# Norm of x moved from VectorE to ScalarE, both heads' first exponentials sent to SBUF, and a new list of order refinements, in an attention plus two-MLP kernel

## The chip, the cores and the metric

The kernel runs on one core of one Trainium2 chip. The metric is device time in microseconds (us) of one execution. Before the change the median of three runs is 991.84 us (990.38 to 995.52).

## What is computed

Causal attention with a decay bias feeds two MLP layers without bias or residual. Batch 4, 8 heads, 576 positions, head dimension 64; the 2304 token rows have 512 columns.

```
scores = q @ k^T / 8 ; bias = -(cum_i - cum_j) ; cum = cumsum(max(s, 0))
scores = where(causal, -1e9, scores + min(bias, 0))
attn   = exp(scores - rowmax) ; attn /= sum(attn) + 1e-9
x      = (attn @ v), heads side by side            # 2304 x 512
h = x @ w_in ; x = (h - tanh(h)) @ w_out           # d_ff 2048
x = ((x @ w_a) * (x @ w_b)) @ w_out2               # d_ff 1536
```

## The kernel before, in words

All large products run in fp16 on TensorE (PE). To keep the precision, an fp32 operand is scaled by a power of two and split into a high and a low fp16 part (`copy_scaled` makes the high one, `lo_part` the low one), and three products stand for one. The scale comes from a norm of the operand: `w_split`, `g_square` and `x_norm` each reduce the squares of a tile to one value for each partition, a tiny matmul with ones adds these up over the partitions, and `pow2` (L735) cuts the result to a power of two with five short VectorE (DVE) instructions.

**Attention** goes by units: one batch and one pair of heads, first with the first two 128-row query tiles (4 x 4 units), then with the last two and the 64-row tail ("merged" units, 4 x 4). In a unit, for each of the two heads `h` and each query tile `t`, `u_qk` (L1002) puts scores into a PSUM bank, a DVE instruction adds the causal mask and takes the row extreme `nm`, `u_exp` (L1045) takes the exponential on ScalarE (ACT) with its row sum `sm`, `u_rec` inverts the sums, and `u_norm` (L1059) scales and splits the result into `a`, which a transposing DMA turns for the product with v. The exponential normally overwrites its PSUM bank. For head 1's first query tile (`t == u.ts[ZSB]`, with `ZSB = 0`) it goes to a tile `zs` in SBUF instead, of which each of the two pools holds two. GpSimd (POOL) cannot be given work on a PSUM bank here, so the flag `ps` in L1068 leaves it out of the choice for `copy_scaled` and `lo_part` where the data stand in PSUM.

**First MLP**: nine blocks of 256 token columns, the first on fp32 weights without a split, the other eight on split operands. At the head of such a block `x_norm` (L1107) finds the norm of the block's x with a DVE instruction (a fused multiply and reduce by max, `sq,xmx`) and four accumulating tiny matmuls, `x_split` makes the fp16 parts, and `gel_scale` (L1125) works out the block's scales (`xc1`, `xt`, `xsg`, `xik`) with short DVE instructions. Then come eight steps of `l1_mm`, `l1_act` (tanh on ACT, the rest on DVE), `l2_mm`. **Second MLP**: `l3_*`, `l4_mm`, and from its third block on a form with seven products for eight (`seven*`), for which `a_sums` and `b_sums` add up sub-matrices into tiles `xf`, `sq`, `x2hl`.

**Order.** Every operation is recorded with a due time (`due`), and a planner (`Plan.run`, L382) issues them engine by engine from its own cost figures. Operations inside `pl.either()` carry several engines, and the planner takes the one that it reckons to be done first; `small` (L926) is such a choice between DVE and POOL. Operations that share a port between POOL and DVE are marked by `shares` and take turns. `REFINE` (L38) is a list of 33 steps; each runs the plan, goes back from its end, and moves the due times towards the latest ones, with random shifts drawn from the step's last number. So a change in any operation or in this list changes the order on all engines.

Of the kernel before, what the change touches and what calls it, by code (L numbers as in the profile page):

```python
# [13 lines left out]
BF16 = mybir.dt.bfloat16  # L14
# [4 lines left out]
AF = mybir.ActivationFunctionType  # L19
ALU = mybir.AluOpType  # L20
# [14 lines left out]
MASKED = -1.0e34  # L35
BLOCKS = [(p, [b]) for p in range(2) for b in range(4)]
TURN = 0.0
REFINE = [(2000.0, 0.1, 300.0, 103), (0.0, 0.2, 1000.0, 287), (0.0, 0.2, 0.0, 206), (400.0, 0.05, 300.0, 66365), (2000.0, 0.1, 300.0, 492), (-200.0, 0.05, 1000.0, 826), (400.0, 0.05, 300.0, 3748), (200.0, 0.2, 1000.0, 456), (-200.0, 0.5, 300.0, 21796), (200.0, 0.0, 300.0, 72166), (0.0, 0.1, 1000.0, 999), (0.0, 0.7, 1000.0, 66510), (2000.0, 0.05, 3000.0, 472), (2000.0, 0.0, 2000.0, 530), (200.0, 0.0, 3000.0, 76843), (100.0, 0.05, 2000.0, 663), (200.0, 0.2, 1000.0, 93186), (0.0, 0.0, 300.0, 851), (100.0, 0.0, 3000.0, 40468), (200.0, 0.2, 0.0, 78025), (2000.0, 0.2, 0.0, 26040), (400.0, 0.05, 2000.0, 38163), (400.0, 0.2, 1000.0, 715), (2000.0, 0.2, 0.0, 319), (2000.0, 0.1, 300.0, 15767), (-200.0, 0.05, 2000.0, 47989), (200.0, 0.2, 0.0, 999), (-200.0, 0.0, 2000.0, 43198), (400.0, 0.05, 0.0, 60058), (200.0, 0.1, 0.0, 58400), (0.0, 0.7, 1000.0, 951), (0.0, 0.2, 1000.0, 27296), (100.0, 0.0, 300.0, 65696)]  # L38
SEVEN = 12
GSB = (1,)  # L40
ZSB = 0
# [590 lines left out]
def tile_attention_two_moes(  # L632
# [20 lines left out]
    KD = DM // P  # L653
# [51 lines left out]
    ones16 = fixed.tile([P, P], BF16, name="ones16")  # L705
# [29 lines left out]
    def pow2(src, n, inv, sc=None):  # L735
        nn = new("moe", [P, 8], F32, "p2n", 4)
        aa = new("moe", [P, 8], I32, "p2a", 4)
        pl.vector.tensor_scalar_max(nn[:, :n], src, TINY)
        pl.vector.tensor_scalar(
            out=aa[:, :n], in0=nn[:, :n].bitcast(I32), scalar1=24, scalar2=23,  # L740
            op0=ALU.logical_shift_right, op1=ALU.logical_shift_left,
        )
        pl.vector.tensor_scalar_mul(inv, aa[:, :n].bitcast(F32), DN)
        if sc is not None:
            bb = new("moe", [P, 8], I32, "p2b", 4)
            pl.vector.tensor_single_scalar(out=bb[:, :n], in_=aa[:, :n], scalar=EXPO, op=ALU.bitwise_xor)
            pl.vector.tensor_scalar_mul(sc, bb[:, :n].bitcast(F32), UP)
# [32 lines left out]
    def lo_part(out_, in_, sc, hi, psum=False):  # L780

        if psum:
            pl.vector.scalar_tensor_tensor(out=out_, in0=in_, scalar=sc, in1=hi, op0=ALU.mult, op1=ALU.subtract)
            return
        with pl.either():
            pl.vector.scalar_tensor_tensor(out=out_, in0=in_, scalar=sc, in1=hi, op0=ALU.mult, op1=ALU.subtract)
            with pl.group():
                if not isinstance(sc, float) or sc != 1.0:
                    pl.gpsimd.tensor_scalar(out=in_, in0=in_, scalar1=sc, scalar2=1.0, op0=ALU.mult, op1=ALU.mult)
                pl.gpsimd.tensor_tensor(out=out_, in0=in_, in1=hi, op=ALU.subtract)  # L790
# [29 lines left out]
    def copy_scaled(out_, in_, sc, psum=False):  # L820
        with pl.either():
            pl.scalar.activation(out=out_, in_=in_, func=AF.Copy, scale=sc)
            pl.vector.tensor_scalar_mul(out_, in_, sc)
            if not psum:
                pl.gpsimd.tensor_scalar(out=out_, in0=in_, scalar1=sc, scalar2=1.0, op0=ALU.mult, op1=ALU.mult)
# [173 lines left out]
    def col(u, h, t):  # L999
        return 2 * u.nq if h == 2 else h * u.nq + u.ts.index(t)  # L1000
# [41 lines left out]
    def span(u, h, t):  # L1042
        return (0, NT + 1) if h == 2 else (u.zoff[t], t + 1)

    def u_exp(u, h, t):  # L1045
        c = col(u, h, t)
        zz = u.ztail if h == 2 else u.pq[h, t]
        to = zz
        if h == 1 and t == u.ts[ZSB]:
            to = u.pq[h, t] = anew(u, [P, (u.ts[ZSB] + 1) * P], F32, "zs")  # L1050
        pl.scalar.activation(
            out=to, in_=zz, func=AF.Exp, scale=-1.0, bias=u.nm[:, c:c + 1], accum_out=u.sm[:, c:c + 1])
# [6 lines left out]
    def u_norm(u, h, t):  # L1059
        c = col(u, h, t)  # L1060
        o, n = span(u, h, t)
        zn = NT + 1 if h == 2 else u.zn
        zz = (u.ztail if h == 2 else u.pq[h, t]).rearrange("p (a c) -> p a c", c=P)
        if h not in u.a:
            u.a[h] = anew(u, [P, zn, 2, P], F16, "am")
        a = u.a[h][:, o:o + n]
        r = u.sm[:, c:c + 1]
        ps = h < 2 and not (h == 1 and t == u.ts[ZSB])  # L1068
        copy_scaled(a[:, :, 0, :], zz, r, ps)
        lo_part(a[:, :, 1, :], zz, r, a[:, :, 0, :], ps)  # L1070
        if o + n == zn:
            u.aT[h] = anew(u, [P, 2 * zn, P], F16, "aTm" if h == 2 else "aT")
            turn(u.aT[h], u.a[h].rearrange("p a e c -> p (a e c)"))
# [33 lines left out]
    def x_norm(blk):  # L1107
        n = blk["n"]
        xf = blk["xf"]
        pn = bank("pv")  # L1110
        acc = new("moe", [P, 1], F32, "xmx", 2)
        sq = new("moe", [P, 1024], BF16, "sq", 2)
        flat = xf.rearrange("p a b -> p (a b)")
        pl.vector.tensor_tensor_reduce(
            out=sq, in0=flat, in1=flat, scale=1.0, scalar=0.0, op0=ALU.mult, op1=ALU.max, accum_out=acc)
        with pl.group():
            for kk in range(KD):
                pl.tensor.matmul(
                    pn[:, 0:1], ones16, acc.bitcast(BF16)[:, 1:2], start=(kk == 0), stop=(kk == KD - 1))
        inv = new("moe", [P, 1], F32, "xinv", 2)  # L1120
        blk["sx"] = new("moe", [P, 1], F32, "xsc", 2)
        pow2(pn[:, 0:1], 1, inv, blk["sx"])
        blk["inv"] = inv

    def gel_scale(blk):  # L1125


        t = new("moe", [P, 4], F32, "xt", 2)
        blk["c1"] = new("moe", [P, C1], F32, "xc1", 2)
        blk["sg"] = new("moe", [P, C1], F32, "xsg", 2)  # L1130
        blk["ik"] = new("moe", [P, 1], F32, "xik", 2)
        pl.vector.tensor_scalar_mul(blk["c1"], inv_in, blk["inv"])
        pl.vector.tensor_tensor(out=t[:, 0:1], in0=blk["inv"], in1=wb, op=ALU.mult)
        pl.vector.tensor_tensor(out=t[:, 1:2], in0=t[:, 0:1], in1=t[:, 0:1], op=ALU.mult)
        pl.vector.tensor_scalar(
            out=t[:, 1:2], in0=t[:, 1:2], scalar1=0.5, scalar2=2.0 ** -8, op0=ALU.mult, op1=ALU.add)
        pl.vector.scalar_tensor_tensor(
            out=t[:, 2:3], in0=t[:, 1:2], scalar=1.0, in1=t[:, 0:1], op0=ALU.min, op1=ALU.mult)
        pl.vector.tensor_single_scalar(
            out=t[:, 2:3].bitcast(I32), in_=t[:, 2:3].bitcast(I32), scalar=EXPMASK, op=ALU.bitwise_and)  # L1140
        pl.vector.reciprocal(t[:, 3:4], t[:, 2:3])
        pl.vector.tensor_scalar_mul(blk["sg"], ro, t[:, 3:4])
        pl.vector.scalar_tensor_tensor(
            out=blk["ik"], in0=t[:, 2:3], scalar=2.0 ** -14, in1=mo, op0=ALU.mult, op1=ALU.mult)

# [418 lines left out]
    start = [START]  # L1564
# [10 lines left out]
    t = 0.0  # L1575
    for j, blk in enumerate(blocks):
# [5 lines left out]
        for i, u in enumerate(us):  # L1582
            t = max(t + STEPM, start[j] - (n - i) * (STEPR if u.merged else STEPF))
# [151 lines left out]
```

## Time and profile before

| | |
|---|---|
| median of 3 runs | 991.84 us (990.38 to 995.52) |
| profiled execution | 993.35 us, span of its instructions 991.6 us |
| PE busy | 914.4 us (92%), granted clock 0.988 of full |
| DVE busy | 816.3 us (82%) |
| ACT busy | 562.6 us (57%) |
| POOL busy | 187.9 us (19%) |

The shares are means over stages with different limits: attention and first MLP run interleaved up to about 600 us, the second MLP after that. In names such as `a<-zs,sm` the left side is written and the right side read; nearly all instructions have the line of the recording helper, L548, so they are told apart by tile names. A duration of one instruction overlaps with its neighbours on an in-order engine, so the distance of starts is shorter than the duration.

### The profile page before, as it was taken

Reading aid. Unit: us, or ns where it says so; the run is one execution under the profiler, and the core shown is the slowest. Engines: PE = TensorE matmul, PEld = TensorE weight load, DVE = VectorE, ACT = ScalarE, POOL = GpSimd, SP = SyncE. Lnnn points to the kernel's source line nnn. Section 1 sums busy time; section 2 is a strip of 40 time slices with the busy share of each in tenths; the row PEclk is TensorE's granted clock in tenths of the full one; section 3 lists DMA queues with packets and bytes.
Section 4 is the critical chain, followed back from the end, with each engine's and each line's share of the span. In section 5 each row is a group of like instructions: output and inputs, shape, how many; then the busy total and the mean of one; then the engine's idle time right before and its main releaser. Section 6 shows DMA issues by size and latency. Waiting matters only on the chain.

```text
span 991.6 us, 21036 instructions
## 1 busy us (share of the span) xinstructions
PE 914.4 (92%) x7998; PEld 689.9 (70%) x7998; DVE 816.3 (82%) x2083; ACT 562.6 (57%) x1111; POOL 187.9 (19%) x271
## 2 busy tenths in 40 slices
PE   1598699999989998999899999999999999999998
PEld 0376588888766776777788877644477777777775
DVE  8999989889999998999899999997257559456554
ACT  6799877758788777887597753332023222212221
POOL 2224221114335313243001010111012002000000
PEclk9999989999998999999999999999999999999999
DMA  8999657357888777796846420200010011001001
GB/s 205 211 331 256 165 95 120 75 121 158 169 165 181 149 140 169 154 190 116 293 139 213 153 83 6 70 11 1 1 54 33 1 44 43 2 1 44 1 1 43
DMA packets 255973, 109.24 MB, mean 110 GB/s; under 512 B 216896, under 2 KB 239664, under 8 KB 255872
## 3 DMA queue, kind: packets, MB, share of 16 engines
q1 hardware_dynamic: 255872, 107.90, 46.0%
q8 instruction: 62, 1.02, 0.4%
q14 instruction: 39, 0.32, 0.1%
HBM read 60.53 MB, written 11.17 MB: 72 GB/s over the span
## 4 chain that ended last, share of the span: by engine, by line
PE 41%; DVE 17%; ACT 3%; DMA 3%; issue 2%; SPq 1%; POOL 1%; DVEq 0%; POOLq 0%; ACTq 0%
PE h L548 15%; PE qk L548 12%; PE acc L548 9%; PE pv L548 6%; DVE w L548 3%; DVE xf L548 2%; DVE ghl L548 2%; DVE qk L548 2%; DMA qkT<-qk 1%; DVE a L548 1%; DVE h L548 1%; SPq L548 1%; DMA x_d<-x2hl 1%; DVE am L548 1%; ACT qk L548 1%
## 5 line engine op out<-in xcount | busy, mean ns | idle before, releaser
L548 PEld LDWEIGHTS <-w 128*128 128x128 f16 x5160 | 499.0, 98 | 130.8 <-issue 25.1
L548 PE MATMUL h<-xhl,w 128*128 128x256 f16 (+1 forms) x2256 | 291.2, 279 | 3.7 <-DVE xhl L548 1.2
L548 PE MATMUL acc<-ghl,w 128*128 128x256 f16 x1536 | 191.3, 274 | 6.4 <-DVE ghl L548 2.8
L548 PE MATMUL h<-xf,w 128*128 128x256 f16 (+1 forms) x560 | 89.1, 308 | 3.4 <-DVE w L548 3.3
L548 PEld LDWEIGHTS <-ghl 128*128 128x128 f16 x432 | 42.2, 98 | 44.6
L548 ACT ACTIVATE sq<-h 128x512 f32<-128x512 f32 x36 | 21.5, 596 | 88.2 <-PE h L548 86.9
L548 DVE CUSTOM_DVE_ANT_0 qk<-qk,caus,cs 128x384 f32<-128x384 f32 (+2 forms) x120 | 64.8, 554 | 2.5 <-PE qk L548 2.3
L548 PE MATMUL acc<-w,ghl 128*128 128x512 f16 x252 | 60.9, 379 | 0.0
L548 PE MATMUL qk<-qkT 128*128 128x128 f16 (+4 forms) x168 | 46.0, 323 | 14.8 <-DVE qkT L548 7.9
L548 ACT ACTIVATE qk<-qk,nm 128x512 f32<-128x512 f32 (+3 forms) x88 | 45.8, 521 | 18.0 <-DVE nm L548 13.2
L548 ACT ACTIVATE th<-h,xc 128x512 f32<-128x512 f32 x64 | 43.5, 680 | 17.3 <-PE h L548 16.1
L548 ACT ACTIVATE w<-w 128x1024 f32<-128x1024 f32 (+1 forms) x44 | 50.6, 1159 | 4.8 <-DMA w<-in_moe_w_b_dram 1.8
L548 DVE SCALAR_TENSOR_TENSOR a<-qk,sm,a 128x512 f16<-128x512 f32 (+3 forms) x88 | 48.2, 571 | 0.3 <-ACT a L548 0.3
L548 PEld LDWEIGHTS <-v 128*64 128x64 f16 x1440 | 37.8, 113 | 14.7 <-issue 11.3
L548 PE MATMUL qk<-kB,qB 67*128 67x128 f16 (+4 forms) x168 | 46.0, 320 | 0.6 <-ACT kB L548 0.4
L548 PE MATMUL qk<-w,ghl 128*128 128x512 f16 x180 | 43.4, 379 | 0.0
L548 ACT ACTIVATE sq<-raw 128x576 bf16<-128x576 f32 (+2 forms) x57 | 38.8, 681 | 7.2 <-DMA raw<-tail_d 4.2
L548 PEld LDWEIGHTS <-qkT 128*128 128x128 f16 (+1 forms) x176 | 17.1, 104 | 34.6 <-DVE qkT L548 13.7
L548 DVE TENSOR_TENSOR g<-g,h 128x512 f32<-128x512 f32 x36 | 24.4, 685 | 20.0 <-PE h L548 19.0
L548 PE MATMUL pv<-aT,v 128*64 128x128 f16 x960 | 34.5, 226 | 6.7 <-DVE p2n L548 3.0
L548 PEld LDWEIGHTS <-sq 128*128 128x128 f16 (+1 forms) x234 | 22.9, 98 | 23.7 <-issue 0.8
L548 DVE SCALAR_TENSOR_TENSOR h<-h,xc,th 128x512 f32<-128x512 f32 x48 | 36.0, 751 | 4.0 <-ACT th L548 3.9
(270 smaller groups left out, 1722.9 us busy)
## 6 DMA issues: line engine op xcount, KB each, us to landing
w<-in_moe_w_out_dram SPq DMA_DIRECT2D x8, 1024.0 KB
w<-in_moe_w_in_dram SPq DMA_DIRECT2D x6, 1024.0 KB
x_d<-x2hl SPq DMA_DIRECT2D x18, 256.0 KB
w<-in_moe_w_a_dram SPq DMA_DIRECT2D x4, 1024.0 KB
xhl<-x_d SPq DMA_DIRECT2D x4, 1024.0 KB
out_dram<-x2f SPq DMA_DIRECT2D x16, 256.0 KB
ws<-in_moe_w_out_dram SPq DMA_DIRECT2D x3, 1024.0 KB
xf<-in_moe_w_b_dram SPq DMA_DIRECT2D x3, 1024.0 KB
```

Source lines behind the costliest of these rows:

```text
L548: return getattr(getattr(plan.nc, name), what)(*[real(a) for a in args], **{k: real(a) for k, a in kw.items()})
```

## The change

`x_norm` sums the squares on ScalarE (Square with an accumulated sum) in place of the DVE reduce, and one tiny matmul stands for four. In `u_exp` and `u_norm` the test `h == 1` becomes `h < 2`, so the first query tile of both heads goes to `zs` in SBUF. Four kinds of short operations in `gel_scale` may go to DVE or POOL. `REFINE` has 33 other steps.

```diff
-REFINE = [(2000.0, 0.1, 300.0, 103), (0.0, 0.2, 1000.0, 287), ...
+REFINE = [(0.0, 0.1, 300.0, 223), (0.0, 0.1, 1000.0, 229), ...
...
-        if h == 1 and t == u.ts[ZSB]:
+        if h < 2 and t == u.ts[ZSB]:
             to = u.pq[h, t] = anew(u, [P, (u.ts[ZSB] + 1) * P], F32, "zs")
...
-        ps = h < 2 and not (h == 1 and t == u.ts[ZSB])
+        ps = h < 2 and not (h < 2 and t == u.ts[ZSB])
...
-        pl.vector.tensor_tensor_reduce(
-            out=sq, in0=flat, in1=flat, scale=1.0, scalar=0.0, op0=ALU.mult, op1=ALU.max, accum_out=acc)
-        with pl.group():
-            for kk in range(KD):
-                pl.tensor.matmul(
-                    pn[:, 0:1], ones16, acc.bitcast(BF16)[:, 1:2], start=(kk == 0), stop=(kk == KD - 1))
+        pl.scalar.activation(out=sq, in_=flat, func=AF.Square, accum_out=acc)
+        pl.tensor.matmul(pn[:, 0:1], ones16, acc.bitcast(BF16)[:, 1:2], start=True, stop=True)
...
-        pl.vector.tensor_scalar_mul(blk["c1"], inv_in, blk["inv"])
-        pl.vector.tensor_tensor(out=t[:, 0:1], in0=blk["inv"], in1=wb, op=ALU.mult)
-        pl.vector.tensor_tensor(out=t[:, 1:2], in0=t[:, 0:1], in1=t[:, 0:1], op=ALU.mult)
-        pl.vector.tensor_scalar(
+        small("tensor_scalar", out=blk["c1"], in0=inv_in, scalar1=blk["inv"], scalar2=1.0, op0=ALU.mult, op1=ALU.mult)
+        small("tensor_tensor", out=t[:, 0:1], in0=blk["inv"], in1=wb, op=ALU.mult)
+        small("tensor_tensor", out=t[:, 1:2], in0=t[:, 0:1], in1=t[:, 0:1], op=ALU.mult)
+        small("tensor_scalar",
             out=t[:, 1:2], in0=t[:, 1:2], scalar1=0.5, scalar2=2.0 ** -8, op0=ALU.mult, op1=ALU.add)
...
-        pl.vector.tensor_scalar_mul(blk["sg"], ro, t[:, 3:4])
+        small("tensor_scalar", out=blk["sg"], in0=ro, scalar1=t[:, 3:4], scalar2=1.0, op0=ALU.mult, op1=ALU.mult)
```

**The norms, in the instruction order.** Where the last two blocks (the 64-row tails in `xtail`, and the last tiles in `xf`) get their norms, DVE's queue reads before the change:

```order
L548 SCALAR_TENSOR_TENSOR ghl_7865<-h_7788,xsg_7255,ghl_7865 128x512
L548 TENSOR_SCALAR xtail_3605<-pv_7893,inv_7271 128x64
L548 ISA sq_7974,xmx_7975<-xtail_3605 128x1024
L548 ISA xmx_7975 128x1
L548 ISA sq_7997,xmx_7998<-xf_7170 128x1024
L548 ISA xmx_7998 128x1
L548 TENSOR_SCALAR p2n_8019<-pv_8000 128x1
```

With the change the same place of DVE's queue has no norm left:

```order
L548 SCALAR_TENSOR_TENSOR ghl_7942<-g_7934,xsg_7208,ghl_7942 128x512
L548 SCALAR_TENSOR_TENSOR x2hl_8025<-x2f_7527,x2hl_8025 128x2x256
L548 TENSOR_SCALAR xtail_3443<-pv_7952,inv_7270 128x64
L548 TENSOR_SCALAR w_0_8050<-xf_7342,wsc_7818 128x4x256
L548 SCALAR_TENSOR_TENSOR w_0_8050<-xf_7342,wsc_7818,w_0_8050 128x4x256
L548 TENSOR_SCALAR p2n_8077<-pv_8063 128x1
```

The two norms have gone to ACT's queue, between the copy of the last attention result to `xf` and the first MLP's tanh:

```order
L548 ACTIVATE x2hl_8025<-x2f_7527 128x2x256
L548 ACTIVATE xf_7221<-pv_7952,inv_7270 128x256
L548 ACTIVATE sq_8037,xmx_8038<-xtail_3443 128x1024
L548 ACTIVATE sq_8060,xmx_8061<-xf_7221 128x1024
L548 ACTIVATE th_8082<-h_7944,xc_5_7080 128x512
```

So a tanh of the block before now stands behind both norms on ACT, and on DVE two parts of a weight split stand in the norms' place.

**POOL, in the instruction order.** At the head of the block before these, POOL's queue holds with the change (`zs` and `z` are exponentials in SBUF, `xt`, `xc` and `xsg` scales of `gel_scale`, the rest operand scaling and splitting):

```order
L548 TENSOR_SCALAR a_6739<-zs_6768,sm_6640 128x3x128
L548 TENSOR_SCALAR am_6828<-z_6693,sm_6640 128x5x128
L548 TENSOR_SCALAR a_6808<-zs_6851,sm_6852 128x3x128
L548 TENSOR_SCALAR qk_7018<-raw_6515,sc_7012 128x9x64
L548 TENSOR_SCALAR cs_7029<-sc_7012,icap_0_130 128x1
L548 TENSOR_SCALAR v_7042<-raw_6515,sc_7012 128x9x64
L548 TENSOR_TENSOR xt_7065<-xt_7065 128x1
L548 TENSOR_SCALAR xc_5_7080<-inv_in_546,xinv_7046 128x8
L548 TENSOR_SCALAR xt_7065<-xt_7065 128x1
L548 TENSOR_TENSOR cs_7029<-inv_7002 128x1
```

Both heads' `zs` are now scaled on POOL, and three of the block's scales wait there behind the 576-wide scaling of `v`; before the change none of the scales of `gel_scale` was on POOL.

## Rows read from the trace of the kernel before

**Rows 1.** The page, part 1: busy time of each engine.

```profile
PE 914.4 (92%) x7998; PEld 689.9 (70%) x7998; DVE 816.3 (82%) x2083; ACT 562.6 (57%) x1111; POOL 187.9 (19%) x271
```

**Rows 2.** Busy time by stretch: us, PE, PEld, DVE, ACT, POOL, clock, DMA.

```profile
0.00:50.00 50.00, 16.45 (x121) 11.02 (x123) 43.73 (x171) 35.03 (x85) 12.99 (x29) 1.00 0.94 210
50.00:480.00 430.00, 396.37 (x4197) 320.78 (x4191) 398.62 (x1211) 341.18 (x727) 132.14 (x203) 0.97 0.76 161
480.00:600.00 120.00, 113.98 (x1047) 100.01 (x1048) 118.50 (x265) 87.46 (x122) 12.09 (x11) 1.00 0.50 172
600.00:991.00 391.00, 387.60 (x2642) 258.09 (x2640) 255.46 (x439) 98.95 (x181) 30.71 (x28) 1.00 0.07 22
```

**Rows 3.** The chain that ended last: the page's shares, then two pieces near 600 us.

```profile
PE 41%; DVE 17%; ACT 3%; DMA 3%; issue 2%; SPq 1%; POOL 1%; DVEq 0%; POOLq 0%; ACTq 0%
PE h L548 15%; PE qk L548 12%; PE acc L548 9%; PE pv L548 6%; DVE w L548 3%; DVE xf L548 2%; DVE ghl L548 2%; DVE qk L548 2%; DMA qkT<-qk 1%; DVE a L548 1%; DVE h L548 1%; SPq L548 1%; DMA x_d<-x2hl 1%; DVE am L548 1%; ACT qk L548 1%
...
596.37 3.61 DVE xf L548 x6
602.17 1.47 PE h L548 x12
```

**Rows 4.** Timeline of DVE at the norm of one block: start, us, instruction.

```profile
421.46 1.21 DVE L548 CUSTOM_DVE_ANT_0 sq<-xf 128x1024 bf16<-128x1024 f32 x1
422.60 0.08 DVE L548 DVE_READ_ACCUMULATOR2_ANT xmx<- 128x1 f32 x1
422.60 0.88 DVE L548 SCALAR_TENSOR_TENSOR am<-z,sm,am 128x640 f16<-128x640 f32 x1
```

**Rows 5.** Groups by shape, ACT: busy us, mean ns, idle before; sums of squares.

```profile
L548 ACT ACTIVATION_READ_ACCUMULATOR sq<-raw 128x1 f32 x57 | 11.1, 194 | 0.0
L548 ACT ACTIVATE sq<-raw 128x1024 bf16<-128x1024 f32 x9 | 9.5, 1058 | 0.0
```

**Rows 6.** Groups by shape, ACT, DVE and POOL: exponentials and their scaling and splitting.

```profile
L548 ACT ACTIVATE zs<-qk,nm 128x384 f32<-128x384 f32 x16 | 9.2, 577 | 2.3 <-DVE nm L548 2.2
L548 ACT ACTIVATE qk<-qk,nm 128x384 f32<-128x384 f32 x16 | 8.7, 547 | 6.1 <-DVE nm L548 3.5 <-DVE xsc L548 1.5 <-DVE sm L548 1.1
...
L548 DVE SCALAR_TENSOR_TENSOR a<-qk,sm,a 128x384 f16<-128x384 f32 x16 | 9.7, 609 | 0.3 <-ACT a L548 0.3
L548 DVE SCALAR_TENSOR_TENSOR a<-zs,sm,a 128x384 f16<-128x384 f32 x14 | 8.5, 609 | 0.1
L548 DVE SCALAR_TENSOR_TENSOR a<-qk,sm,a 128x128 f16<-128x128 f32 x16 | 5.4, 340 | 0.0
L548 DVE SCALAR_TENSOR_TENSOR a<-zs,sm,a 128x128 f16<-128x128 f32 x12 | 4.2, 353 | 0.0
L548 DVE TENSOR_SCALAR a<-qk,sm 128x384 f16<-128x384 f32 x5 | 3.1, 613 | 0.0
L548 DVE TENSOR_SCALAR a<-qk,sm 128x128 f16<-128x128 f32 x5 | 1.7, 348 | 0.1
...
L548 POOL TENSOR_SCALAR a<-zs,sm 128x384 f16<-128x384 f32 x9 | 5.3, 584 | 18.4 <-DMA kB<-part_d 10.4 <-ACT qkT L548 5.2 <-DMA qkT<-qk 1.3
L548 POOL TENSOR_TENSOR a<-zs,a 128x384 f16<-128x384 f32 x2 | 2.0, 980 | 0.2
```

**Rows 7.** Groups by shape, DVE and POOL: short operations, and the low part of v.

```profile
L548 DVE SCALAR_TENSOR_TENSOR v<-raw,sc,v 128x576 f16<-128x576 f32 x8 | 6.7, 832 | 0.0
L548 DVE TENSOR_TENSOR xt<-xt 128x1 f32<-128x1 f32 x8 | 2.0, 244 | 0.0
...
L548 DVE TENSOR_SCALAR xt<-xt 128x1 f32<-128x1 f32 x8 | 1.1, 141 | 0.0
...
L548 POOL TENSOR_TENSOR cs<-inv 128x1 f32<-128x1 f32 x16 | 3.3, 208 | 8.0 <-DVE kB L548 2.9 <-DVE qk L548 2.9 <-DVE v L548 1.2
```

**Rows 8.** Waits of PE: waiting line <- releaser: us in total, times, longest.

```profile
PE pv L548 <- DVE xmx L548: 4.2, 1, 4.2
PE acc L548 <- DVE a L548: 3.7, 3, 1.9
```

More of the change, by code (lines that the diff above doesn't have):

```diff
@@ L37 @@
 TURN = 0.0
-REFINE = [(2000.0, 0.1, 300.0, 103), (0.0, 0.2, 1000.0, 287), (0.0, 0.2, 0.0, 206), (400.0, 0.05, 300.0, 66365), (2000.0, 0.1, 300.0, 492), (-200.0, 0.05, 1000.0, 826), (400.0, 0.05, 300.0, 3748), (200.0, 0.2, 1000.0, 456), (-200.0, 0.5, 300.0, 21796), (200.0, 0.0, 300.0, 72166), (0.0, 0.1, 1000.0, 999), (0.0, 0.7, 1000.0, 66510), (2000.0, 0.05, 3000.0, 472), (2000.0, 0.0, 2000.0, 530), (200.0, 0.0, 3000.0, 76843), (100.0, 0.05, 2000.0, 663), (200.0, 0.2, 1000.0, 93186), (0.0, 0.0, 300.0, 851), (100.0, 0.0, 3000.0, 40468), (200.0, 0.2, 0.0, 78025), (2000.0, 0.2, 0.0, 26040), (400.0, 0.05, 2000.0, 38163), (400.0, 0.2, 1000.0, 715), (2000.0, 0.2, 0.0, 319), (2000.0, 0.1, 300.0, 15767), (-200.0, 0.05, 2000.0, 47989), (200.0, 0.2, 0.0, 999), (-200.0, 0.0, 2000.0, 43198), (400.0, 0.05, 0.0, 60058), (200.0, 0.1, 0.0, 58400), (0.0, 0.7, 1000.0, 951), (0.0, 0.2, 1000.0, 27296), (100.0, 0.0, 300.0, 65696)]
+REFINE = [(0.0, 0.1, 300.0, 223), (0.0, 0.1, 1000.0, 229), (2000.0, 0.1, 1000.0, 187), (100.0, 0.05, 0.0, 709), (200.0, 0.05, 1000.0, 473), (200.0, 0.05, 3000.0, 361), (400.0, 0.2, 2000.0, 946), (100.0, 0.05, 0.0, 45006), (200.0, 0.05, 1000.0, 549), (0.0, 0.1, 1000.0, 4418), (-200.0, 0.0, 300.0, 717), (0.0, 0.0, 3000.0, 517), (400.0, 0.05, 0.0, 79456), (0.0, 1.0, 1000.0, 49811), (100.0, 0.2, 2000.0, 6575), (0.0, 0.0, 3000.0, 417), (200.0, 0.1, 3000.0, 457), (200.0, 0.05, 0.0, 388), (2000.0, 0.0, 2000.0, 54115), (-200.0, 0.2, 1000.0, 361), (100.0, 0.05, 300.0, 580), (2000.0, 0.1, 300.0, 81259), (2000.0, 0.0, 3000.0, 71620), (400.0, 0.1, 0.0, 448), (2000.0, 0.05, 0.0, 482), (200.0, 0.2, 0.0, 2108), (400.0, 0.1, 3000.0, 38295), (400.0, 0.1, 300.0, 998), (100.0, 0.05, 1000.0, 881), (2000.0, 0.5, 3000.0, 496), (-200.0, 0.05, 0.0, 66801), (2000.0, 0.5, 3000.0, 671), (400.0, 0.05, 2000.0, 77269)]
 SEVEN = 12
```

## The prediction

> **What bounds the kernel now.** I read the busy shares first. PE is busy 92% and DVE 82% [rows 1], but these are means over unlike stages, so the table of stretches comes next [rows 2]. From 600 us on PE is busy 387.6 of 391 us so PE alone sets the pace and no saving on another engine can shorten that part. The reader should look at the two rows before it. From 50 to 480 us DVE is busy 398.6 of 430 us (93%), and from 480 to 600 us 118.5 of 120 us (99%), while PE leaves 33.6 and 6.0 us idle there. ACT is busy 341.2 and 87.5 us (79% and 73%), POOL 132.1 and 12.1 us (31% and 10%). So DVE is the fullest engine of the first 600 us. The chain of waits says the same: DVE holds 17% of the span, ACT 3%, POOL 1%, and the last pieces before PE becomes solid are DVE's, six sums into `xf` from 596.4 us [rows 3]. PE's total work is fixed by the matmuls, so the end of the kernel moves by as much as PE's idle time before 600 us moves, and most of that idle time is DVE's doing. With the first 50 us (33.6 us idle, start-up) left out, there are 39.6 us of PE idle time to win at most. That is the ceiling, and DVE's work is the handle.
>
> **The change part by part.** Durations are those of the profiled execution, 993.35 us with a span of 991.6 us, which lies 1.5 us above the median of 991.84. On an in-order queue I count the distance of starts, which is about 0.07 us less than a duration.
>
> *Norms.* Eight norms leave DVE. One takes 421.46 to 422.60 us there until the next instruction starts, 1.14 us [rows 4]: 8 x 1.14 = **9.1 us off DVE**. ACT gets eight squares of 128x1024 with an accumulator read, 1.058 + 0.194 = 1.25 us each [rows 5], 10.0 us. 24 matmuls of one column go; they cost PE some hundredths of a microsecond each, and I count them as nothing, since PE waits at that place for DVE anyway (the one wait on `xmx` is 4.2 us [rows 8]). Before and after, a norm lies on the way to a block's head and takes 1.1 to 1.3 us, so its own latency hardly changes; what is queued ahead of it does, on ACT in place of DVE.
>
> *First exponentials to SBUF.* 32 exponentials (16 of 128 and 16 of 384 columns) write `zs` in place of PSUM. That costs ACT 577 - 547 = 30 ns each [rows 6], 1 us in all. The scaling and splitting that follow may now go to POOL, and the instruction order shows by how much they do. High parts: DVE had ten on `qk` and three on `zs`, and now has eight on `zs`, all of 128 columns: 5 x 613 + 5 x 348 ns go and five of at most 348 come, so 3.1 us less. Low parts on DVE: 32 on `qk` go (16 x 609 + 16 x 340 = 15.2 us) and 23 on `zs` come (10 x 609 + 13 x 353 = 10.7 us), 4.5 us less [rows 6]. Together 7.6 us in 14 fewer instructions, or **6.6 us off DVE** by distances of starts. ACT loses 21 high parts of at most 0.6 us, some 10 us, which pays for the norms: ACT ends within 2 us of where it was. POOL gets 26 high parts of at most 584 ns and nine more low parts, each a scaling and a subtraction of at most 0.59 + 0.98 us [rows 6]: at most 15 + 14 us, and by the mix of sizes some 25 us. It gives other work back, mainly the low parts of `v`, of which DVE takes five more at 0.832 us [rows 7]: **3.8 us onto DVE**. A PSUM bank is also free after the exponential rather than after both parts; PE's waits on `a` for a bank, 3.7 us [rows 8], are what that can win, and I count it in the range alone. What could take it back are the `zs` tiles: two in each pool, as before, for twice the use.
>
> *Scales.* 21 short operations of `gel_scale` go from DVE to POOL, at 141 to 244 ns each by the two kinds shown [rows 7]. By distances of starts 0.07 to 0.17 us: 1.5 to 3.6 us, and I take **2.5 us off DVE**. On POOL the nearest row has 208 ns [rows 7], so the time there is small; the price is a change of engine, and that POOL's queue stands ahead (next part).
>
> *New refinement steps.* All orders move. The instruction order counts 2085 DVE instructions before and 2039 after; 16 of the 46 are norms, 14 parts of `a`, 21 scales, and five `v` come back. The other kinds that change engine by the new order put about 1 us on DVE. Ahead of the last GELU step of the first MLP stand 1620 DVE rows before and 1554 now: 66 fewer, where 46 leave in all. So 20 more go behind it, into the stage where DVE is only 255.5 of 391 us busy [rows 2]. At DVE's mean of 816.3 / 2083 = 0.39 us [rows 1] that is worth up to 8 us, which I take for the low end only, since what is put off may be wanted soon.
>
> *Sum.* 9.1 + 6.6 + 2.5 - 3.8 - 1 = 13.4 us off DVE. DVE is busy 517.1 of the 550 us from 50 to 600 us [rows 2], 94%, so I let 94% of it through: 12.6 us. 993.35 - 12.6 = 980.8, so **981 us**. Against the median of 991.84 this is 1.1% less. What is late next is PE itself, with two thirds of its 39.6 us idle time left.
>
> **The port of DVE and POOL.** At this place the trace can speak against the change. A low part on `qk` reads one operand from SBUF, the same on `zs` reads two. Of DVE's two-operand SBUF instructions the tiny `xt<-xt` takes 244 ns where its one-operand sister takes 141 [rows 7], so something holds these up by about 0.1 us. Yet at 384 columns the parts on `zs` and on `qk` take 609 ns alike, and at 128 columns 353 and 340 [rows 6]: 0 to 13 ns, with POOL at 31%. By these rows the 23 new ones lose 0.2 us, and the sum stays. The Trainium skill (SBUF — State Buffer, Who interferes with whom) says that a DVE instruction with two SBUF inputs contends with a GpSimd instruction that reads SBUF, and that whoever comes second is blocked for the whole of the other. By that rule the sum would lose what the next paragraph's first rival loses; the trace bears out a hold-up in the tiny operations and hardly any in the long ones.
>
> **The rivals.**
>
> *DVE stands behind POOL (slower).* POOL takes on some 25 us of new work on `zs` and 21 short operations of about 0.21 us, 4 us: 29 us that read SBUF. If DVE, being full, stood through all of it, it would lose 29 us where it gains 13.4: 993.35 + 15.6 = 1009 us. It decides from 13.4 of the 29 us on, and is slower beyond what a measurement tells from about 18 of 29. For it: the 0.1 us on tiny operations. Against it: the equal 609 ns, POOL's low share, and that POOL gives work back. The same end is reached if a block's scales, now on POOL behind operand work, come late. Chance 0.12, near 1000 us where it happens.
>
> *The room is not used (same).* PE's idle time before 600 us does not hang on DVE's total but on chains (transposing DMAs, the block heads, the two `zs` tiles), and the new order only moves idle time from PE's waits on DVE to its waits on ACT, which now holds the norms in its queue. DVE would show 13 us more idle time and the end stay: 989 to 995 us. For it: DVE stands at 93%, not 99%, from 50 to 480 us, and the order is new in every place. Against it: ACT keeps 89 us free in that stretch and PE's long waits there name DVE. Chance 0.20.
>
> *More than the sum (faster).* The 20 further DVE instructions behind the first MLP count in full, 8 us, and banks come free earlier: 993.35 - 13.4 - 8 = 972 us. PE's 39.6 us idle would allow it. Chance 0.13.
>
> *The forecast*, 973 to 987 us: 0.55.
>
> **How the numbers follow.** A measurement of this kernel tells 0.5% from no change, so 986.9 and 996.8 us are the bounds. Faster: forecast and the better case, 0.55 + 0.13 = 0.68. Same: 0.20. Slower: 0.12. The range should leave out no more than 2 in 10: it reaches down to 971, which takes in the better case, and up to 993, which takes in most of the second rival; outside remain the rival on the port and the edges of the others.
>
> **What would show it.** Right: DVE's busy time in the page near 803 us with about 46 fewer instructions; the point where PE becomes solid, now 602 us, some 12 us earlier; PE's idle time from 50 us to that point down from 39.6 to about 27 us; the low parts on `zs` still near 609 ns. Wrong by the port: those parts and other two-operand DVE instructions longer by tenths of a microsecond, or DVE idle with POOL as releaser. Wrong by chains: DVE with more idle time, and PE's waits on ACT's norms, on POOL's scales or on `zs` in the list of waits. If PE's stage after 600 us is longer than now, the new order has put first-MLP work into it and my point of comparison is at fault.

## The result, and the profile after

| | before | after |
|---|---|---|
| median | 992.84 us (990.38 to 995.52, 4 runs) | 980.1 us (979.71 to 980.5, 4 runs) |
| ratio | | 0.9876, 95% interval 0.9851 to 0.9900 |
| span of the profiled execution | 991.6 us | 978.3 us |

The changed kernel is 1.24% faster (12.3 us by the ratio, 12.7 us between the medians): 980.1 us, where 981 us was forecast. The page of the changed kernel begins (busy time of each engine, then the chain of waits by engine):

```profile
PE 910.9 (93%) x7974; PEld 688.0 (70%) x7974; DVE 805.9 (82%) x2037; ACT 565.9 (58%) x1114; POOL 199.0 (20%) x313
...
PE 58%; DVE 17%; ACT 4%; SPq 3%; DMA 3%; issue 3%; POOL 0%; ACTq 0%; DVEq 0%; POOLq 0%
```

DVE has 46 instructions fewer and 10.4 us less busy time than in [rows 1], ACT 3.3 us more, POOL 11.1 us more, PE 3.5 us less.

The stage before PE becomes solid has to be compared up to the right instant, which the chain of waits gives: the last pieces of DVE ahead of the long run of PE. Before, these stood at 596 and 602 us [rows 3]; in the changed kernel:

```profile
587.79 2.40 DVE xf L548 x4
590.58 1.47 PE h L548 x12
```

So PE becomes solid 11.6 us earlier (590.6 for 602.2). Busy time by stretch (us, PE, PEld, DVE, ACT, POOL, clock, DMA) of the kernel before, cut at that instant:

```profile
50.00:602.00 552.00, 512.29 (x5254) 421.81 (x5249) 519.11 (x1478) 429.56 (x849) 144.23 (x214) 0.98 0.70 163
602.00:991.00 389.00, 385.66 (x2630) 257.07 (x2629) 253.46 (x436) 98.03 (x178) 30.71 (x28) 1.00 0.07 23
```

and of the kernel after, with the start-up ahead of it:

```profile
0.00:50.00 50.00, 16.97 (x130) 11.33 (x130) 42.89 (x172) 36.72 (x85) 11.61 (x28) 1.00 0.92 214
50.00:590.00 540.00, 511.40 (x5246) 422.66 (x5247) 506.61 (x1430) 429.38 (x850) 157.85 (x260) 0.98 0.72 166
590.00:978.00 388.00, 382.52 (x2598) 254.03 (x2597) 256.40 (x437) 99.83 (x180) 29.54 (x26) 1.00 0.07 23
```

The reader should see three things. PE issues nearly the same number of matmuls between 50 us and the cut, 5254 and 5246, although the 24 norm matmuls that went had stood there; so the later stretch holds no less of the other work, and it is 12 us shorter. PE's idle time in it falls from 552.0 - 512.3 = 39.7 us to 540.0 - 511.4 = 28.6 us. And DVE's share of it does not move: 519.1 of 552 us is 94.0%, 506.6 of 540 is 93.8%. DVE was as full as before and had 12.5 us less to do. Behind the cut the stage is no longer than before (388 us for 389), though the chain passes through DVE and ACT twice more there, from 729 to 732 us and at 939 us.

Groups by shape of DVE after the change (busy us, mean ns, idle before):

```profile
L548 DVE SCALAR_TENSOR_TENSOR a<-zs,sm,a 128x384 f16<-128x384 f32 x24 | 15.7, 660 | 0.8 <-POOL a L548 0.8
L548 DVE SCALAR_TENSOR_TENSOR a<-zs,sm,a 128x128 f16<-128x128 f32 x25 | 8.7, 353 | 0.1
L548 DVE TENSOR_SCALAR a<-zs,sm 128x128 f16<-128x128 f32 x8 | 2.3, 283 | 0.1
L548 DVE TENSOR_TENSOR sq<-xhl 128x512 f32<-128x512 f16 x13 | 10.3, 794 | 0.0
```

The low parts on `zs` at 384 columns take 660 ns in the mean, 51 more than in [rows 6]; at 128 columns they stay at 353. `sq<-xhl`, a sum of two SBUF operands in the second MLP, took this before:

```profile
L548 DVE TENSOR_TENSOR sq<-xhl 128x512 f32<-128x512 f16 x12 | 8.2, 686 | 0.5 <-DMA xhl<-x_d 0.5
```

These means mislead; the single instructions show why. Of the 24 low parts at 384 columns 21 take 601 to 619 ns, as before. The other three take 730, 790 and 1496 ns, and each of them began while an instruction of POOL was running. Of the 13 `sq<-xhl` 11 take 0.68 to 0.69 us and two take 1.41 us. One of each kind, with POOL's instruction beside it (start, us):

```profile
323.21 0.79 DVE L548 SCALAR_TENSOR_TENSOR a<-zs,sm,a 128x384 f16<-128x384 f32 x1
322.80 0.80 POOL L548 TENSOR_SCALAR am<-z,sm 128x640 f16<-128x640 f32 x1
...
677.28 1.41 DVE L548 TENSOR_TENSOR sq<-xhl 128x512 f32<-128x512 f16 x1
676.98 1.16 POOL L548 TENSOR_TENSOR x2hl<-xhl 128x512 f32<-128x512 f16 x1 [4.06 <-DVE xf L548]
```

An instruction of DVE that takes over 60 ns more than the median of its kind and shape over all runs is called a hold-up below, and what it takes beyond the median is its cost. There are 57 in the kernel before (17.3 us in all) and 46 in the changed one (16.8 us), and every one of them has an instruction of POOL beside it. Low parts that read `qk` from PSUM are not held up: 24 before and 16 after began with over 0.25 us of a POOL instruction still to run, and none took 10 ns more than its median. Low parts on `zs` that began so were held up in the changed kernel in all four cases, before in one of two.

ACT and POOL after the change:

```profile
L548 ACT ACTIVATE sq<-xf 128x1024 bf16<-128x1024 f32 x7 | 7.4, 1055 | 0.2
L548 ACT ACTIVATION_READ_ACCUMULATOR sq<-xf 128x1 f32 x7 | 1.3, 187 | 0.0
```

```profile
L548 POOL TENSOR_SCALAR a<-zs,sm 128x384 f16<-128x384 f32 x24 | 14.0, 587 | 30.4 <-DVE sm L548 8.6 <-ACT qk L548 5.1 <-DVE qkT L548 4.3
L548 POOL TENSOR_TENSOR xt<-xt 128x1 f32<-128x1 f32 x6 | 1.2, 194 | 14.1 <-DVE p2n L548 11.6 <-DVE xhl L548 2.5
L548 POOL TENSOR_TENSOR cs<-inv 128x1 f32<-128x1 f32 x11 | 4.4, 404 | 7.9 <-DVE sm L548 3.6 <-DVE qk L548 3.0 <-DVE p2n L548 1.2
```

A norm costs ACT 1.06 + 0.19 us, as the rows of other squares had it [rows 5]. A short scale takes 194 ns on POOL; but POOL's own two-operand `cs<-inv` went from 208 ns [rows 7] to 404 in the mean: six of the eleven take 0.19 to 0.20 us, and five, each beside a running instruction of DVE, take 0.49 to 0.76 us. Of PE's waits after the change, these four bear on the rivals (total, times, longest):

```profile
PE pv L548 <- ACT sq L548: 8.5, 5, 4.9
PE h L548 <- ACT xhl L548: 3.0, 1, 3.0
PE acc L548 <- DVE a L548: 4.0, 2, 2.9
PE qk L548 <- ACT zs L548: 1.7, 3, 0.9
```

The first of them was longer before the change:

```profile
PE pv L548 <- ACT sq L548: 15.7, 8, 4.7
```

All of it, before and after, is on squares of the weights and of q, k and v, which ACT did already; no tiny matmul of a norm of x waits for ACT in the changed kernel. A wait on the split behind a norm on ACT (3.0 us) has come, the one on `xmx` [rows 8] is gone, and the wait on `a` is where it was.

### The profile page after: what moved, and what is told of

It reads as the page before. It is cut to its first block, busy times and chain, and to the rows that moved or that the text cites. A ratio compares the mean times of both kernels' runs of the same rounds, so it can differ in the third digit from the quotient of the medians.

```text
span 978.3 us, 20996 instructions
## 1 busy us (share of the span) xinstructions
PE 910.9 (93%) x7974; PEld 688.0 (70%) x7974; DVE 805.9 (82%) x2037; ACT 565.9 (58%) x1114; POOL 199.0 (20%) x313
## 4 chain that ended last, share of the span: by engine, by line
PE 58%; DVE 17%; ACT 4%; SPq 3%; DMA 3%; issue 3%; POOL 0%; ACTq 0%; DVEq 0%; POOLq 0%
PE h L548 22%; PE acc L548 16%; PE qk L548 14%; PE pv L548 7%; DVE w L548 3%; SPq L548 3%; DVE xf L548 2%; DVE qk L548 2%; DMA qkT<-qk 1%; DVE ghl L548 1%; DVE a L548 1%; DVE g L548 1%; DVE x2f L548 1%; DVE h L548 1%; DVE xhl L548 1%
## 5 line engine op out<-in xcount | busy, mean ns | idle before, releaser
L548 PE MATMUL acc<-ghl,w 128*128 128x256 f16 x1536 | 188.4, 274 | 4.8 <-DVE ghl L548 3.5
L548 ACT ACTIVATE bits<-h,cpc 128x512 f32<-128x512 f32 x18 | 12.4, 687 | 50.0 <-DVE g L548 31.0
L548 DVE TENSOR_TENSOR g<-sq 128x256 f32<-128x256 f32 x36 | 14.8, 422 | 30.6 <-ACT sq L548 30.4
L548 PEld LDWEIGHTS <-qkT 128*128 128x128 f16 (+1 forms) x176 | 16.7, 104 | 32.5 <-DVE qkT L548 17.3
L548 DVE TENSOR_TENSOR g<-g,th 128x256 f32<-128x256 f32 x35 | 15.4, 441 | 28.8 <-ACT th L548 28.7
```

What stands on the lines that cost most here:

```text
L548: return getattr(getattr(plan.nc, name), what)(*[real(a) for a in args], **{k: real(a) for k, a in kw.items()})
```

## The experiments

Two questions were open. Does DVE's work really set the time, or is it the new order? And which of the parts pays? The first six experiments below keep the changed kernel's order on every engine, instruction by instruction, and alter only what is issued at a given place; the planner does not know of it. The other six let the planner make a new order. All ratios are against the kernel before, run on the same chip; 0.1% is 1 us. Differences between two ratios carry about 0.3% of uncertainty.

| run | what | median us | ratio, 95% interval |
|---|---|---|---|
| after | the change | 980.1 | 0.9876 (0.9851 to 0.9900) |
| e3_norm_dve | norms back on DVE, same order | 990.8 | 0.9976 (0.9962 to 0.9990) |
| e4_dve_extra | more DVE work, same order | 993.72 | 1.0009 (0.9995 to 1.0023) |
| e10_act_extra | more ACT work, same order | 985.39 | 0.9917 (0.9898 to 0.9936) |
| e11_pool_read | more POOL work, same order | 987.99 | 0.9948 (0.9930 to 0.9966) |
| e13_head0_dve | POOL's share of head 0 on DVE, same order | 986.16 | 0.9948 (0.9930 to 0.9967) |
| e14_scales_dve | scales back on DVE, same order | 981.62 | 0.9896 (0.9873 to 0.9920) |
| s0_before_66 | old code, a third list | 1015.91 | 1.0218 (1.0194 to 1.0241) |
| s1_norms_66 | norms alone, a third list | 1018.65 | 1.0235 (1.0207 to 1.0262) |
| s2_zs_66 | zs alone, a third list | 1017.56 | 1.0230 (1.0203 to 1.0257) |
| s4_all_66 | all code edits, a third list | 1005.09 | 1.0105 (1.0080 to 1.0129) |
| e8_before_bare | old code, no list | 1059.02 | 1.0694 (1.0658 to 1.0730) |
| e9_after_bare | all code edits, no list | 1066.51 | 1.0756 (1.0730 to 1.0783) |

### Norms back on DVE, order kept

```diff
 pl.scalar.activation(out=sq, in_=flat, func=AF.Square, accum_out=acc)      # planned as this
+# issued in its place: nc.vector.tensor_tensor_reduce(..., op0=mult, op1=max, accum_out=acc),
+# and four accumulating matmuls in place of the one behind it
```

> The changed kernel's order on all engines is kept, but at each of the eight norms DVE gets the old multiply-and-reduce and PE the old four matmuls in place of ACT's square. DVE work goes up by 8 x 1.14 = 9.1 us, ACT work goes down by 10 us. Theory (DVE's work ahead of 600 us is the handle, 94% of it goes through): 980.1 + 8.6 = 988.7 us, between 985 and 992. Rival (the new order made the gain and DVE has room): 979 to 982 us.

```profile
PE 913.0 (92%) x7998; PEld 688.7 (70%) x7998; DVE 814.5 (82%) x2053; ACT 557.2 (56%) x1098; POOL 198.9 (20%) x313
...
L1127 DVE CUSTOM_DVE_ANT_0 sq<-xf 128x1024 bf16<-128x1024 f32 x7 | 9.0, 1280 | 0.1
```

Measured: 0.9976, that is 1.0% or about 10 us slower than the change, for 8.6 us more DVE busy time and 8.7 us less on ACT. The theory's number held (990.8 us in a range of 985 to 992). DVE had no room for these 9 us, although ACT was relieved by as much.

### More work on DVE alone, order kept

```diff
 pl.scalar.activation(out=sq, in_=flat, func=AF.Square, accum_out=acc)
+# issued beside it: nc.vector.tensor_reduce(out=junk_a, in_=flat, axis=X, op=max)
```

> The changed kernel's order is kept, ACT's squares stay, and beside each of them DVE gets one more reduce over 1024 columns whose result nobody reads (the output is the same). DVE work goes up by about 9 us and nothing else changes. Theory (DVE's work is the handle): 985 to 992 us, the same as with the norms on DVE. Rival (room on DVE): 979 to 982 us. If this run is slower than the norms on DVE by over 2 us, ACT's relief counts too.

```profile
PE 915.6 (92%) x7974; PEld 690.4 (70%) x7974; DVE 814.2 (82%) x2045; ACT 566.1 (57%) x1114; POOL 199.0 (20%) x313
...
L1128 DVE TENSOR_REDUCE junk_a<-xf 128x1 f32<-128x1024 f32 x7 | 8.5, 1214 | 0.2 <-ACT xf L548 0.2
```

Measured: 1.0009, about 13 us slower than the change for 8.3 us of DVE work: 1.6 us for each. That is above the range. The 3 us between this run and the one before it may be the ACT norms, which this one keeps; but the instruction on DVE is another one, so that is not shown. The next run puts the question to ACT directly.

### More work on ACT, order kept

```diff
 pl.scalar.activation(out=sq, in_=flat, func=AF.Square, accum_out=acc)
+# issued a second time, the same instruction
```

> The changed kernel's order is kept and each norm's square is done twice on ACT: 10 us more ACT work ahead of 600 us, and 1.25 us more latency at each of eight block heads. Theory (DVE is the handle, ACT has room): 980 to 984 us. Rival (the norm has made ACT's queue the new wait): 988 to 991 us.

```profile
PE 914.4 (93%) x7974; PEld 689.5 (70%) x7974; DVE 806.2 (82%) x2037; ACT 574.7 (58%) x1130; POOL 199.0 (20%) x313
...
PE pv L548 <- ACT sq L548: 11.5, 7, 4.7
PE pv L548 <- ACT sq L1127: 2.9, 4, 1.2
```

Measured: 0.9917, about 4 us slower than the change for 8.8 us more on ACT. This lies between theory and rival: the time grows by less than half of what is put on ACT, where for DVE it was all and more. The 2.9 us at L1127, at four of the eight doubled norms, are the waits that the edit has made. The 11.5 us are on other squares, and stand at 11.0 us in the run with the norms back on DVE. As the second square also makes each block head later, this run does not tell ACT's load from that latency.

### More work on POOL, order kept

```diff
 copy_scaled(a[:, :, 0, :], zz, r, ps)
+# where POOL has been chosen: the same gpsimd.tensor_scalar issued a second time (42 times in all)
```

> The changed kernel's order is kept and each of POOL's 42 scalings of zs into the high part is done twice: about 20 us more POOL work that reads SBUF. Theory (POOL has room, its port costs DVE little): 980 to 984 us, with the low parts on zs on DVE below 700 ns at 384 columns. Rival (DVE stands behind POOL at their port): 990 to 1000 us, with DVE's two-operand instructions longer by tenths of a microsecond.

```profile
PE 912.6 (93%) x7974; PEld 687.6 (70%) x7974; DVE 811.1 (82%) x2037; ACT 567.4 (58%) x1114; POOL 221.0 (22%) x355
...
L548 DVE SCALAR_TENSOR_TENSOR a<-zs,sm,a 128x384 f16<-128x384 f32 x24 | 16.8, 706 | 4.8 <-POOL a L1083 4.7
...
DVE a L548 <- POOL a L1083: 6.5, 11, 1.5
```

Measured: 0.9948, about 7 us slower than the change for 22.0 us more on POOL. Theory and rival both missed: it is between them. Two costs can be read off. DVE's busy time rose by 5.2 us with not one instruction more: there are 60 hold-ups for 46, and they cost 22.1 us for 16.8, which is the whole rise. The mean of the low parts on `zs` at 384 columns goes from 660 to 706 ns by them, while their median is 619 ns for 610; again not one hold-up is without an instruction of POOL beside it. And DVE waited 6.5 us for the second copy. The first is the hold-up between DVE and POOL that the prediction asked for; the second is plain lateness. A twin of this run with POOL instructions that only write was not run, so the two are told apart by these rows alone.

### POOL's share of head 0 given to DVE, order kept

```diff
 copy_scaled(a[:, :, 0, :], zz, r, ps)
 lo_part(a[:, :, 1, :], zz, r, a[:, :, 0, :], ps)
+# head 0's first query tile, where POOL has been chosen: issued as vector.tensor_scalar
+# (21 times) and vector.scalar_tensor_tensor (5 times)
```

> The changed kernel's order is kept and its zs tiles too, but what POOL does for head 0's first query tile (21 high parts, five low parts) is issued on DVE instead: the part of the change that only SBUF allowed is undone. DVE gets 26 instructions, 8.6 to 11 us by rows of 283 to 613 ns; POOL loses some 17 us. Theory (DVE is the handle, at the 1.0 to 1.2 us for each us that the norms on DVE have shown): 988 to 993 us. Rival (zs helps by early PSUM banks, or not at all): 979 to 982 us.

```profile
PE 912.7 (93%) x7974; PEld 687.4 (70%) x7974; DVE 815.6 (83%) x2063; ACT 567.6 (58%) x1114; POOL 183.7 (19%) x282
...
L1080 DVE TENSOR_SCALAR a<-zs,sm 128x384 f16<-128x384 f32 x13 | 7.9, 608 | 0.1
L1080 DVE TENSOR_SCALAR a<-zs,sm 128x128 f16<-128x128 f32 x8 | 2.9, 358 | 0.0
L548 DVE SCALAR_TENSOR_TENSOR a<-zs,sm,a 128x384 f16<-128x384 f32 x24 | 14.8, 625 | 0.0
```

Measured: 0.9948, about 7 us slower than the change, for 9.7 us more DVE busy time and 15.3 us less on POOL. A little under the range of the theory, and far from the rival: the PSUM banks are still freed early here, yet the time is lost. In this order, what `zs` brings is work for POOL. The two means that differ from the change's are single hold-ups again: two of the 24 low parts at 384 columns are held up here for three there (625 ns for 660), and of the eight high parts at 128 columns one takes 866 ns, beside an instruction of POOL, and the others 276 to 330. So the second multiply by one, with which the high parts were issued here, costs nothing that shows: the single multiply takes 275 to 287 ns in the changed kernel.

### Scales back on DVE, order kept

```diff
 small("tensor_scalar", out=blk["c1"], ...)      # and the other four in gel_scale
+# where POOL has been chosen: the same instruction issued on vector (21 in all)
```

> The changed kernel's order is kept, but the 21 short operations of the block scales that went to POOL are issued on DVE instead. DVE gets about 3.2 us, POOL loses about 5 us, and some changes of engine on the way to a block's tanh go. Theory (DVE is the handle): 982 to 984 us. Rival (on POOL the scales come late, and the way of the scales is what counts): 976 to 980 us.

```profile
PE 908.3 (93%) x7974; PEld 685.4 (70%) x7974; DVE 808.0 (83%) x2058; ACT 565.4 (58%) x1114; POOL 196.0 (20%) x292
```

Measured: 0.9896, 0.2% above the change, which the intervals don't tell from it. By DVE busy time the scales are worth 2.1 us; neither theory nor rival is excluded. In the profiled execution PE's idle time is 2.2 us longer than the change's (69.6 us of the span for 67.4), but PE is busy 2.6 us less with the same 7974 matmuls, at a granted clock of 0.996 for 0.990, and this hides it.

### Old code, parts and all edits under a third list

To compare codes under one treatment, the old and the new list were put one after the other, 66 steps, and a step was kept only where the plan's own end came earlier.

```diff
+        best = self.run()
         for gap, mix, shake, seed in steps:
-            self.move(self.backward(self.run(), gap), mix, shake, seed)
+            # move, run; if the plan's end is not earlier, put the due times back
```

> The code of the kernel before, ordered by a third list: the old and the new list one after the other, 66 steps, each kept only where the plan's end comes earlier. DVE has 2086 instructions, as before. Theory (DVE's work decides, the list matters little): 990 to 996 us, as the kernel before. Rival (the new list made the gain): up to 10 us below the kernel before.

> The kernel before with the norms of x on ACT alone, ordered by the same 66 steps with the same rule. DVE has 21 instructions fewer than with the old code under these steps; by counts and durations of the rows about 8 us less DVE work in all, but some 7 us more ahead of the first MLP's last GELU step. Theory (DVE's total is the handle): 8 us below the old code under the same steps. Second form of it (what lies ahead of the last GELU step is the handle): no gain. Rival (the list): within 2 us of the old code under the same steps.

> The kernel before with both heads' first exponentials in SBUF alone, ordered by the same 66 steps with the same rule. DVE has 7 instructions fewer, DVE work by counts within 1 us of the old code under these steps: what POOL takes of zs it gives back elsewhere. Theory (DVE's total is the handle): within 2 us of the old code under the same steps. Rival (PSUM banks freed early are what helps): 4 us or more below it.

> All code edits of the change, ordered by the same 66 steps with the same rule, in place of the change's own list. DVE has 38 instructions fewer than the old code under these steps, and by counts about 12.6 us less DVE work in all and ahead of the last GELU step alike. Theory (the code edits make the gain): 9 to 14 us below the old code under the same steps, 979 to 985 us. Rival (the change's own list made it): within 3 us of the old code under the same steps.

Busy time of the old code, of the norms alone, of `zs` alone and of all edits, in this order:

```profile
PE 922.3 (91%) x7998; PEld 690.3 (68%) x7998; DVE 823.3 (81%) x2084; ACT 558.7 (55%) x1102; POOL 199.1 (20%) x277
```

```profile
PE 923.1 (91%) x7974; PEld 693.0 (68%) x7974; DVE 815.9 (80%) x2063; ACT 566.5 (56%) x1124; POOL 183.8 (18%) x271
```

```profile
PE 921.0 (91%) x7998; PEld 691.1 (68%) x7998; DVE 825.8 (81%) x2077; ACT 554.7 (55%) x1106; POOL 191.4 (19%) x288
```

```profile
PE 916.2 (91%) x7974; PEld 689.8 (69%) x7974; DVE 812.4 (81%) x2046; ACT 564.8 (56%) x1111; POOL 194.9 (19%) x313
```

Busy time from the start to the end of the tanh of the first MLP's last GELU step, in the same order (us, PE, PEld, DVE, ACT, POOL, clock, DMA):

```profile
0.00:599.24 599.24, 517.33 (x5217) 418.49 (x5218) 548.64 (x1613) 447.79 (x902) 165.87 (x247) 0.97 0.72 166
```

```profile
0.00:606.95 606.95, 520.90 (x5217) 423.58 (x5218) 555.67 (x1615) 460.78 (x932) 157.04 (x247) 0.97 0.73 164
```

```profile
0.00:601.26 601.26, 515.38 (x5209) 418.76 (x5210) 556.56 (x1618) 449.35 (x916) 158.94 (x258) 0.97 0.70 165
```

```profile
0.00:589.52 589.52, 511.28 (x5190) 417.61 (x5191) 535.93 (x1576) 455.59 (x914) 165.35 (x287) 0.98 0.74 169
```

The level was missed: the old code came to 1015.9 us, 22 us above the same code under its own list, with 7.0 us more DVE busy time (823.3 for 816.3). So a list is worth as much as the whole change, and more. Under equal treatment all edits together give 1.0105 / 1.0218 = 0.989, 10.8 us, with 10.9 us less DVE busy time: what the theory said, on a worse level. The norms alone, with 7.4 us less DVE busy time, gave nothing (2.7 us slower, within the intervals). That is against the theory's first form, in which DVE's total counts, and what its second form said: up to the last GELU step DVE has 7.0 us more to do than with the old code, 555.7 for 548.6, and the step ends 7.7 us later. With all edits it has 12.7 us less, and the step ends 9.7 us earlier. In all four runs DVE is busy 91 to 93% of that time, so a late step and much work before it go together in these rows; what speaks for the second form is that its 7 us were counted before the run. The rival of the list, within 2 us of the old code, fits the norms alone as well. `zs` alone gave nothing either, as the theory said and the rival of early PSUM banks did not; DVE has 7.9 us more to do ahead of the step, which ends 2.0 us later. The scales alone were not run.

### Old and new code without a list

> The code of the kernel before with an empty list of refinement steps: the planner's first order. DVE has 2113 instructions. Together with the new code under an empty list it tells what the code edits are worth without any list. No theory gives the level; with a list made for another search the same code came to 1016 us, so 1010 to 1050 us.

> All code edits of the change with an empty list of refinement steps. By counts and durations DVE has 11.8 us less work than the old code under an empty list. Theory (the code edits make the gain, through DVE's work): 8 to 14 us below the old code under an empty list. Rival (the list made the gain): within 3 us of it.

Both have `REFINE = []`. The page's busy times, the stretch from 50 to 600 us and PE's waits on `zs`, of the old code:

```profile
PE 927.0 (88%) x7998; PEld 689.7 (65%) x7998; DVE 844.6 (80%) x2111; ACT 566.5 (54%) x1124; POOL 136.9 (13%) x213
...
50.00:600.00 550.00, 482.27 (x4928) 390.76 (x4929) 512.64 (x1444) 409.67 (x822) 100.51 (x167) 0.97 0.68 159
...
PE qk L548 <- ACT zs L548: 2.4, 5, 1.2
```

and of the new:

```profile
PE 935.3 (88%) x7974; PEld 696.0 (65%) x7974; DVE 833.5 (78%) x2092; ACT 564.8 (53%) x1117; POOL 149.9 (14%) x242
...
50.00:600.00 550.00, 480.14 (x4840) 389.06 (x4839) 493.75 (x1403) 403.77 (x813) 113.05 (x194) 0.95 0.66 158
...
PE qk L548 <- ACT zs L548: 8.3, 6, 3.2
PE pv L548 <- DMA aT<-a: 6.6, 3, 3.1
```

The old code lies above the 1010 to 1050 us that were expected. Here the theory failed: with 11.1 us less DVE busy time in all (833.5 for 844.6) the new code is 7.5 us slower. The stretch shows how. DVE is busy 493.8 of 550 us, 90%, where the old code has 512.6, 93%: it waits more. PE's waits on exponentials in `zs` rise from 2.4 to 8.3 us, and a wait on transposed `a` of 6.6 us is among PE's largest. This is the rival in which the room isn't used: less work for DVE, and an order that leaves the difference idle. It is not the whole of it: PE is busy 8.3 us longer, 935.3 us for 927.0 with 24 matmuls fewer, at a mean granted clock of 0.971 for 0.984, and the two profiled executions lie 12.3 us apart.

## Why the prediction was right

**What bounds.** DVE's work ahead of the solid stage set the time, as forecast: its share of that stage stayed at 94% while its work fell by 12.5 us and the stage by 12. Putting the norms' work back in the same order cost 10 us for 8.6. The predicted time came out (981 us, measured 980.1), and so did three of the signs named for it: 46 instructions fewer, solid 11.6 us earlier for "some 12", PE's idle time 28.6 us for "about 27". Two did not: DVE's busy time is 805.9 us for "near 803", and the low parts on `zs` take 660 ns in the mean for "near 609", though their median is about 610 ns before and after. One premise holds only in part, that the end moves by as much as PE's idle time. Between the profiled executions PE's idle time fell by 9.8 us and its busy time by 3.5; and over the runs with the same 7974 matmuls in this order PE's busy time goes from 908.3 us (granted clock 0.996) to 915.6 us (0.988).

**Norms.** Sized at 9.1 us off DVE, of which 94% goes through, 8.6 us; measured by the reverse edit, 10 us with some 3 of uncertainty. ACT was to end within 2 us of where it was in busy time, and ends 3.3 us above. That ACT's own load would cost nothing was too simple: 8.8 us more of it, which also came as latency at the block heads, cost about 4 us.

**First exponentials to SBUF.** Sized at 6.6 us off DVE less 3.8 us for the `v` parts that come back, a net 2.8; the traces have 6.8 and 3.7 us without the hold-ups. The reverse edit with the order kept costs 7 us, which has no such return. The early PSUM banks, left to the range, brought nothing that shows: PE's wait on `a` is 4.0 us for 3.7.

**The terms that were mis-sized.** DVE's busy time fell by 10.4 us and not by 13.4. Added up by kinds, without the hold-ups, the norms took off 9.3 us. The scales took off 1.5, where 2.5 was in the sum, and the other kinds that changed engine by the new order put on 4.0, where "about 1" was in it. Hold-ups cost 0.5 us less.

**Port.** The prediction priced it at 0.2 us, and in all it cost nothing more: 16.8 us of hold-ups for 17.3. But it read the rows as a small cost on every instruction, and the cost is a large one on a few: its "about 0.1 us" on the tiny `xt<-xt` is the mean of six that took 142 to 151 ns and two that took 441 and 633. The Trainium skill (SBUF — State Buffer, Who interferes with whom) calls the port pair that the two engines share an exclusive lock. The trace agrees: in the four held-up low parts on `zs` and the two `sq<-xhl`, what DVE took beyond the median was the rest of POOL's instruction less 0.14 to 0.21 us. The run with POOL's copies doubled shows it again: 14 more hold-ups, and 5.2 us of DVE time for 22 us of POOL. The rival's 1009 us was far off because DVE does not stand through all of POOL's work, only where such instructions meet, and because POOL as a whole took on little: 157.9 of 540 us ahead of the cut, 29%, for 144.2 of 552 us, 26%.

**New list.** The prediction gave the 20 further instructions behind the last GELU step nothing in the sum, and that was right: they still run before PE is solid, with 437 DVE instructions behind the cut for 436. There DVE has 256.4 us for 253.5, and 2.2 of these 2.9 us are hold-ups (6.3 us for 4.1). Ahead of the cut, start-up included, the hold-ups fell from 13.2 to 10.5 us. So DVE's busy time ahead of the cut fell by 13.3 us, where the sum has 13.4: the terms that were mis-sized, some 3 us too little on DVE, were made up for by 2.7 us of hold-ups that went, which the prediction did not foresee. That the sum came out within a microsecond is in part luck.

**What the prediction did not see** is how much the list carries. It treated the orders as equally good with a chance of 0.20 that the room is not used. The three pairs give for the code edits 12.3 us (own lists), 10.8 us (the third list) and -7.5 us (no list). By these the mechanism needs an order that fills DVE up to the solid stage; and the norms alone under the third list speak for DVE's work ahead of the last GELU step as what counts, not its total. That a microsecond off DVE is about a microsecond off the kernel is shown within the change's own order, and beyond it by the pair under the third list alone.

**What stays open.** How the 12.3 us divide between the code and its list: neither the old code under the new list nor the new code under the old one was run. And how much one would keep with each part alone and a list searched for it: single parts under the third list gave nothing, and one list tells little, since lists differ by 20 us. The reverse edits add up to 10 + 7 + 2 = 19 us, more than the gain; they put 8.6 + 9.7 + 2.1 = 20.4 us back on DVE, while the work that the change puts on DVE, 3.7 us of `v` parts and 4.0 of other kinds, stays there. So they are prices within this order and no division of the gain.

## What to carry to other kernels

Where one engine is 94% busy up to an instant at which another becomes solid, take that instant from the chain of waits and compare work and idle time up to it, not shares of the whole span: in this kernel, with the order kept, work put back on the full engine ahead of it came into the time nearly one to one or more. Moving work to an engine with room is not free: here a microsecond on ACT at the block heads cost about half of one and a microsecond on POOL about a third, POOL partly by holding up single operations of DVE. Where a mean has grown, look at the single instructions before pricing it: a few that are held up look like a small cost on all. And an edit in a kernel with a planned order is worth what the order makes of it, so compare codes under orders that have had the same search, and expect the search to weigh as much as the edit.

## What was not expected of the hardware

What DVE and POOL lose to each other falls on a few instructions, and heavily. In the changed kernel a low part of 384 columns that reads both operands from SBUF took 601 to 619 ns, or, where it began with over 0.25 us of a POOL instruction still to run, 730 to 1496; one that reads PSUM took at most 16 ns more than its median in any run. Doubling POOL's copies from SBUF made DVE 5.2 us busier with the same 2037 instructions, by 60 hold-ups for 46. And DVE held POOL up in turn: five of POOL's eleven one-column `cs<-inv` took 0.49 to 0.76 us beside a running instruction of DVE, the other six 0.19 to 0.20 us.
